# Attention windows fetched in eight-row transfers, and the next batch's transposes and scores placed after the last slot's values

## The chip, the core and the metric

The kernel runs on one core of a Trainium2 chip. Its time is device time in microseconds (us) from the start to the end of the program on that core. The engines are named as the profile names them: PE (TensorE, matrix multiplications; PEld is its weight load), DVE (VectorE), ACT (ScalarE), POOL (GpSimd), SP (SyncE). Every engine works through its own instructions in order. Transfers ("DMAs") are issued by POOL, SP or ACT and carried out by 16 DMA engines that all of them share.

## The reference

Two stages follow each other. First, chunked attention over 4 batches, 8 heads, 768 tokens and a head size of 64. The tokens are cut into chunks of 32; the queries of a chunk see 8 memory keys and values of the batch, plus a window of up to 56 tokens: 16 to the left of the chunk, the chunk, 8 to the right.

```python
scores = scale * np.matmul(q_c, k_full.transpose(0, 1, 3, 2))
a = np.exp(scores - max); a = a / sum(a)
out[:, :, c_start:c_end] = np.matmul(a, v_full)
```

Second, a mixture of 8 experts over the 3072 resulting rows of 512. Two linear maps of a row give noisy logits, the two best experts are chosen, their weights are the softmax of the two logits, and each chosen expert computes `relu(x @ w1) @ w2` with `w1` 512 x 1024 and `w2` 1024 x 512. The result is a 3072 x 512 float32 array.

## The kernel before

Everything is computed in bfloat16 with float32 accumulation; POOL's transfers convert the float32 inputs on the way in.

**Attention** goes through the 4 batches, and through 3 slots for each batch (`i` from 0 to 11, `tp` is the slot within the batch); a slot is 256 tokens, eight chunks. For a batch `b`:

- `load_nat` (L117) loads q, k or v of the batch, one POOL transfer of 768 KB each, into the tiles `nat` (q and k) and `vn` (v). `spread_v` (L368) reorders v into `vp` with two POOL copies. `window_v` then issues from SP a transfer of `vp` to a scratch area `vd` in device memory (L374), and from POOL two transfers of the memory values (L378, 8 partitions each) and four of the windows (L383): for each of two head parities 32 and then 24 window rows. In the resulting tile `vb` the partition is the place in the window (8 memory rows, then 56 window rows; the parities at partitions 0 and 64), so that each of the 24 chunks has its values ready as one operand. A window transfer reads 512-byte pieces of `vd`, since every token occurs in up to two windows.
- `turn` (L393) makes one of eight units of transposed q or k: 12 small PE transposes into a PSUM bank, then a copy to `qT` or `kT` by ACT or DVE. Copies of the four q units are on ACT; the four k units alternate between ACT and DVE (L549).
- `scores` (L408, L415) are 40 matmuls into one PSUM tile `ps_s`, then a row maximum and a subtraction on DVE (L423, L425). `exps` is the exponential on ACT (L430).
- `turn_p` transposes the probabilities on PE and copies them on ACT (L436, L439); `values` computes the row sums (L447) and the weighted values (L453) on PE, and divides on DVE (L457, L460). `turn_x` (L470, L472) and `gate` (L480, L482) are the transposes of the result and the logits; `keep_x` (L485) stores the rows to the area `xd` from ACT.

PE, ACT, DVE and SP follow an order written out by hand, POOL keeps program order. The order in slot `i` is: `scores(i+1)`, `turn_p(i)`, `turn_x(i-1)`, `values(i)`, `exps(i+1)`, `gate(i-1)`, then a part of the routing. A table `PLAN` and the function `fill` put the eight units of the next batch into this: for the first batch all behind the second slot, for the others two q units before that slot's `values` and the rest behind it. Thus the units of the next batch precede the last slot of the current one. At the first slot of a batch POOL issues the window of the next batch, q and k of the one after, the spread of its v, and the load of the v after that.

There is one tile for all experts' weights, `w_all`, 8 places of 16 KB per partition. Attention's buffers (`xrow`, `vn`, both `vb`, four `nat`) lie in the last places, from which an expert is loaded only after attention. The first three experts are loaded by POOL during the last slots (`load_expert`, L78 and L79). Two POOL transfers cannot share one of eight completion counters at the same time, so in the built code each POOL transfer waits for the one issued eight transfers before it, where nothing else already made sure of that.

**Routing and experts.** After the last slot a chain of small DVE, PE and POOL operations sorts the tokens into lists by expert pair. POOL gathers the rows of each list (L671), PE turns the first ones (L691), and then runs all expert matmuls (L714 first layer, L726 second) up to the end, with results scattered to the output by POOL (L677). Other experts' weights are loaded during this stage.

Of the kernel before, what the change touches and what calls it, by code (L numbers as in the profile page):

```python
# [22 lines left out]
def kernel(  # L23
# [40 lines left out]
    w_all = wpool.tile([128, E, WE], BF16, name="w_all")  # L64
    wflat = w_all.rearrange("p e c -> p (e c)")
    w1v = w_all[:, :, 0:KP * F].rearrange("p e (k f) -> p e k f", k=KP)
    w2v = w_all[:, :, KP * F:WE].rearrange("p e (f d) -> p e f d", f=FB)
# [9 lines left out]
    def load_expert(e):  # L77
        pin(nc.gpsimd.dma_start(out=w1v[:, e], in_=moe_w1[e].rearrange("(kp p) f -> p kp f", p=128)))  # L78
        pin(nc.gpsimd.dma_start(out=w2v[:, e], in_=moe_w2[e].rearrange("(fb p) d -> p fb d", p=128)))  # L79


    def load_part(e, i):
        h = slice(i % 2 * KP // 2, (i % 2 + 1) * KP // 2) if i < 2 else slice(i % 2 * FB // 2, (i % 2 + 1) * FB // 2)
        if i < 2:
            pin(nc.gpsimd.dma_start(out=w1v[:, e, h], in_=moe_w1[e].rearrange("(kp p) f -> p kp f", p=128)[:, h]))
        else:
            pin(nc.gpsimd.dma_start(out=w2v[:, e, h], in_=moe_w2[e].rearrange("(fb p) d -> p fb d", p=128)[:, h]))
# [14 lines left out]
    scol = [E * WE]  # L102
# [6 lines left out]
    vb = [scratch(2 * NCH * HP * D).rearrange("p (a c w) -> p a c w", a=2, c=NCH) for _ in range(2)][::-1]  # L109
# [261 lines left out]

    def window_v(b):
        t, o = vb[b % 2], vd[b % 2]
        nc.sync.dma_start(out=o[LC:LC + S, :].rearrange("(p s) c -> p (s c)", s=SO), in_=vp)  # L374
        for par in range(2):
            p0 = par * 64
            cols = slice(par * 256, (par + 1) * 256)
            pin(nc.gpsimd.dma_start(out=t[p0:p0 + NM, par], in_=mvn[b * NM:(b + 1) * NM, cols].unsqueeze(1).to_broadcast([NM, NCH, 256])))  # L378
        for par in range(2):
            p0 = par * 64  # L380
            cols = slice(par * 256, (par + 1) * 256)
            for r0, n in ((0, CH), (CH, WIN - CH)):
                pin(nc.gpsimd.dma_start(out=t[p0 + NM + r0:p0 + NM + r0 + n, par],  # L383
                                        in_=o[r0:r0 + S, cols].rearrange("(c k) w -> k c w", k=CH)[0:n]))
# [131 lines left out]
    with tc.manual_schedule(engines={ET.PE, ET.Activation, ET.DVE, ET.SP}):  # L516
# [10 lines left out]
        spread_v(0)  # L527
        window_v(0)
# [3 lines left out]
        load_v(1)  # L532
        load_kq(1)
        spread_v(1)
# [16 lines left out]
        def fill(i, at):  # L551
            b, tp = divmod(i, TP)
            if b + 1 < B:
                turns(b + 1, PLAN[min(b, 1)].get((tp, at), ()))

# [6 lines left out]
        for i in range(NT):  # L562
# [35 lines left out]
            if last:  # L598
                break
# [386 lines left out]
```

## Time and profile before

| what | us |
|---|---|
| median of 3 runs (lowest, highest) | 363.06 (361.42, 363.59) |
| the profiled execution's own time | 358.42 |
| span of its instructions | 356.7 |
| PE, DVE, ACT, POOL busy | 285.9, 170.3, 136.9, 134.3 |
| start of the last slot's values | 124.51 |
| start of the first expert matmul | 144.14 |

The profiled execution has its own time: it is one run, and the span in its trace leaves out 1.7 us around the instructions. All places in the trace are given in us from the start of the span. A row of a timeline reads: start, duration of the group, engine, line, operation, output <- input, form, how many; in brackets the idle time of that engine just before and what ended it. The table of stretches gives for each stretch of time the busy time of each engine with the number of instructions, the granted PE clock as a share of full speed, the mean share in which the DMA engines had a packet in hand (over 1 where packets overlap) and the GB/s that arrived.

### The profile page before, as it was taken

The page shows a single profiled execution, that of the slowest core. Times are in us where ns is not written, and L with a number is a line of the kernel's source. Part 1 is how long each engine was busy: PE and PEld are TensorE (multiplying, and loading weights), DVE is VectorE, ACT ScalarE, POOL GpSimd, SP SyncE. Part 2 cuts the span into 40 slices and gives each one's busy share as a digit, 9 for nine tenths or more (in the row PEclk, how much of TensorE's full clock was granted, in tenths as well). Part 3 has the DMA queues.
Part 4 walks back from the last instruction along what each step waited for, and adds up shares of the span by engine and source line. Part 5 has one row for each costly group of instructions (what it writes and reads, how often), then busy time and mean ns, then how long its engine had stood idle before and what let it go on. Part 6 is the DMA issues. An engine that isn't in the chain of part 4 may idle for free.

```text
span 356.7 us, 7042 instructions
## 1 busy us (share of the span) xinstructions
PE 285.9 (80%) x2934; PEld 186.3 (52%) x2955; DVE 170.3 (48%) x349; ACT 136.9 (38%) x189; POOL 134.3 (38%) x181
## 2 busy tenths in 40 slices
PE   0356577777847732999999999999999999999991
PEld 0245455666736621865544465664455775565540
DVE  7656456699689885531133302954310334223221
ACT  8813645564645610144322343213243222243310
POOL 6460573354453036706530744332580122201122
PEclk9995655565687865699999999999999999999998
DMA  8999999999999999499999999961289971100012
GB/s 122 235 171 169 245 174 208 251 198 211 247 156 208 253 249 180 106 194 143 178 196 235 209 173 252 159 119 51 87 166 189 208 184 54 53 2 2 25 47 81
DMA packets 49866, 56.97 MB, mean 160 GB/s; under 512 B 16931, under 2 KB 39523, under 8 KB 49828
## 3 DMA queue, kind: packets, MB, share of 16 engines
q0 software_dynamic: 34240, 46.82, 73.2%
q1 hardware_dynamic: 13920, 6.62, 10.9%
q10 hardware_dynamic: 1668, 3.02, 2.4%
q8 instruction: 25, 0.41, 0.5%
q14 instruction: 13, 0.11, 0.1%
HBM read 70.39 MB, written 13.96 MB: 236 GB/s over the span
## 4 chain that ended last, share of the span: by engine, by line
PE 33%; issue 20%; POOL 5%; DVE 4%; DMA 3%; POOLq 1%; ACT 0%; DVEq 0%
PE p_h L714 18%; PE p_y L726 13%; POOL out_dram L677 4%; DMA out_dram<-y,main_dst 1%; DMA xTt<-xt 1%; DMA xt<-xd,main_src 1%; POOL xt L671 1%; DVE w_all L460 1%; PE p_xt L691 0%; POOL w_all L844 0%; POOLq L981 0%; DVE mx L423 0%; DVE sc L425 0%; ACT xT L472 0%; PE ps_o L453 0%
## 5 line engine op out<-in xcount | busy, mean ns | idle before, releaser
L714 PE MATMUL p_h<-xTt,w_all 128*128 128x256 bf16 (+3 forms) x669 | 102.7, 313 | 0.7 <-DVE xTt L692 0.5
L726 PE MATMUL p_y<-w_all,h 128*128 128x512 bf16 x446 | 102.3, 379 | 0.9
L714 PEld LDWEIGHTS <-w_all 128*128 128x128 bf16 x736 | 70.0, 101 | 36.3 <-issue 0.7
L702 ACT ACTIVATE h<-p_h 128x512 bf16<-128x512 f32 (+1 forms) x81 | 44.7, 551 | 95.9 <-PE p_h L714 88.3
L726 PEld LDWEIGHTS <-h 128*128 128x128 bf16 x464 | 45.3, 98 | 51.6
L700 DVE TENSOR_SCALAR h<-p_h 128x512 bf16<-128x512 f32 (+1 forms) x49 | 31.0, 633 | 82.8 <-PE p_h L714 73.7
L677 POOL DMA_INDIRECT out_dram<-y,main_dst x28 | 30.9, 1103 | 87.9 <-DVE y L732 75.4
L732 DVE SCALAR_TENSOR_TENSOR y<-p_y,main_w,y 128x512 f32<-128x512 f32 x28 | 21.0, 750 | 39.2 <-PE p_y L726 32.5
L393 PE MATMUL p_t<-identb,w_all 128*64 128x128 bf16 x384 | 20.6, 288 | 23.0 <-DMA w_all<-in_k_dram 13.4
L671 POOL DMA_INDIRECT xt<-xd,main_src x28 | 27.9, 997 | 24.2 <-DMA xTt<-xt 13.0
L730 ACT ACTIVATE y<-p_y,main_w 128x512 f32<-128x512 f32 x28 | 19.2, 687 | 37.0 <-PE p_y L726 36.0
L393 PEld LDWEIGHTS <-w_all 128*64 128x64 bf16 x384 | 18.1, 155 | 25.2 <-DMA w_all<-in_k_dram 13.9
L439 ACT COPY pT<-p_p 128x1024 bf16<-128x1024 bf16 x12 | 12.1, 1012 | 27.5 <-PE p_p L436 27.5
L383 POOL DMA_DIRECT2D w_all<-vd x16 | 11.8, 747 | 23.8 <-DMA vd<-vp 19.3
L460 DVE TENSOR_TENSOR w_all<-ps_o,rs 128x512 bf16<-128x512 f32 x24 | 15.6, 686 | 8.2 <-PE ps_o L453 7.8
L415 PE MATMUL ps_s<-kT,qT 128*32 128x112 bf16 x384 | 11.6, 276 | 7.2 <-DVE kT L549 5.4
L368 POOL COPY vp<-w_all 128x1536 bf16<-128x1536 bf16 x8 | 11.5, 1469 | 13.2 <-DMA w_all<-in_v_dram 13.2
L430 ACT ACTIVATE pb<-sc 128x1024 bf16<-128x1024 f32 x12 | 12.8, 1063 | 8.9 <-DVE sc L425 8.7
L549 DVE COPY kT<-p_t 64x768 bf16<-64x768 bf16 x12 | 11.5, 955 | 7.9 <-PE p_t L393 7.8
L425 DVE TENSOR_TENSOR sc<-ps_s,mx 128x1024 f32<-128x1024 f32 x12 | 14.7, 1225 | 0.8
L423 DVE TENSOR_REDUCE mx<-ps_s 128x16 f32<-128x1024 f32 x12 | 14.7, 1224 | 0.8 <-PE ps_s L415 0.5
L453 PE MATMUL ps_o<-w_all,pT 128*32 128x128 bf16 x384 | 10.9, 280 | 3.3 <-issue 2.0
(172 smaller groups left out, 284.0 us busy)
## 6 DMA issues: line engine op xcount, KB each, us to landing
w_all<-in_moe_w_dram POOLq DMA_DIRECT2D x16, 1024.0 KB, 20.7
w_all<-in_moe_w_dram POOLq DMA_DIRECT2D x8, 512.0 KB, 13.8
w_all<-in_v_dram POOLq DMA_DIRECT2D x4, 768.0 KB, 12.1
w_all<-in_k_dram POOLq DMA_DIRECT2D x4, 768.0 KB, 20.9
w_all<-in_q_dram POOLq DMA_DIRECT2D x4, 768.0 KB, 18.1
vd<-vp SPq DMA_DIRECT2D x4, 768.0 KB, 9.0
w_all<-vd POOLq DMA_DIRECT2D x8, 384.0 KB, 13.0
w_all<-vd POOLq DMA_DIRECT2D x8, 288.0 KB, 13.3
```

The lines of the kernel that those rows point to most:

```text
L393: nc.tensor.transpose(out=p_t[own(par), s, :], in_=src[:, 2 * pair + par, s * D:(s + 1) * D], identity=identb, tile_position=(0, par * 64))
L423: nc.vector.tensor_reduce(out=mx, in_=s3, axis=AX, op=Alu.max)
L425: nc.vector.tensor_tensor(out=sc, in0=s3, in1=bc(mx, KW), op=Alu.subtract)
L460: nc.vector.tensor_tensor(out=xr[:, j, 0:Dm].rearrange("p (h d) -> p h d", h=H), in0=ps_o[:, j].rearrange("p c a d -> p (c a) d"), in1=bc( ...
L671: i = nc.gpsimd.indirect_dma_start(out=xts[key].bitcast(I32), out_offset=None, in_=xd, in_offset=bass.IndirectOffsetOnAxis(ap=ix, axis=0))
L677: i = nc.gpsimd.indirect_dma_start(out=out, out_offset=bass.IndirectOffsetOnAxis(ap=ix, axis=0), in_=y, in_offset=None, bounds_check=N - 1 ...
L700: nc.vector.tensor_scalar(out=out_, in0=in_, scalar1=0.0, scalar2=None, op0=Alu.max)
L702: nc.scalar.activation(out=out_, in_=in_, func=Act.Relu)
L714: nc.tensor.matmul(out=o, lhsT=w(kp * F + f * 128, 128), rhs=x[:, kp], start=(kp == 0), stop=(kp == KP - 1))
L726: nc.tensor.matmul(out=p, lhsT=h[:, (f * n + j) * 128:(f * n + j + 1) * 128], rhs=w(KP * F + f * Dm, Dm), start=(f == 0), stop=(f == FB - 1))
L730: nc.scalar.activation(out=y, in_=p, func=Act.Copy, scale=weight)
L732: nc.vector.scalar_tensor_tensor(out=y, in0=p, scalar=weight, in1=y, op0=Alu.mult, op1=Alu.add)
```

## The change

Four things change together.

- **Window transfers.** The four window transfers of a batch become 14. Each takes, for one parity, eight rows that lie seven partitions apart (row `x`, `x+7`, ... `x+49` of the window). The transfer of `vp` to `vd` is no longer a part of `window_v`: it follows the spread directly, a batch ahead of its windows.
- **Order on POOL.** The q of the next batch is issued after six of the 14 window transfers, its k after the last. The load of v for the second batch moves ahead of the first window.
- **Places.** Both `vb` tiles become tiles of their own (`w_b`), in which the weights of the last three experts are put later; the remaining attention buffers move to places 2 to 4 of a five-place `w_all`.
- **Order on PE, ACT and DVE.** In the last slot of a batch (`edge`), `scores(i+1)` is no longer at the top. After `values(i)` come `gate(i-1)`, all eight units of the next batch, `scores(i+1)` and `exps(i+1)`. `PLAN` and `fill` are gone. The load of the third expert moves behind the last units.

```diff
-    w_all = wpool.tile([128, E, WE], BF16, name="w_all")
+    EA = E - 3
+    w_all = wpool.tile([128, EA, WE], BF16, name="w_all")
+    w_b = [wpool.tile([128, 3, WP], BF16, name=f"w_b{i}") for i in range(2)]
+    places = [(w_all[:, e, 0:WP], w_all[:, e, WP:WE]) for e in range(EA)]
+    places += [(w_b[2 * x // 3][:, 2 * x % 3], w_b[(2 * x + 1) // 3][:, (2 * x + 1) % 3]) for x in range(3)]
...
-            for r0, n in ((0, CH), (CH, WIN - CH)):
-                pin(nc.gpsimd.dma_start(out=t[p0 + NM + r0:p0 + NM + r0 + n, par],
-                                        in_=o[r0:r0 + S, cols].rearrange("(c k) w -> k c w", k=CH)[0:n]))
+    XW = WIN // 8
+    def spans_v(b, lo, hi):
+        o = vd[b % 2]
+        for x in range(lo, hi):
+            for par in range(2):
+                p0 = par * 64 + NM + x
+                src = bass.AP(tensor=o.tensor, offset=o.offset + x * Dm + par * 256, ap=[[XW * Dm, 8], [CH * Dm, NCH], [1, 256]])
+                pin(nc.gpsimd.dma_start(out=vb[b % 2][p0:p0 + 7 * XW + 1:XW, par], in_=src))
+    def window_v(b):
+        memory_v(b)
+        spans_v(b, 0, 3)
+        if b + 1 < B:
+            load_nat(nat[(b + 1) % 2][1], q, b + 1)
+        spans_v(b, 3, XW)
+        if b + 1 < B:
+            load_nat(nat[(b + 1) % 2][0], k, b + 1)
...
         spread_v(0)
+        copy_v(0)
+        load_v(1)
         window_v(0)
...
-        load_v(1)
-        load_kq(1)
         spread_v(1)
+        copy_v(1)
         load_v(2)
...
             if tp == 0 and more:
                 window_v(b + 1)
                 if b + 2 < B:
-                    load_kq(b + 2)
                     spread_v(b + 2)
+                    copy_v(b + 2)
...
-            if not last:
+            if not (last or edge):
                 sc = scores(i + 1)
...
             xrs[i] = values(i, pTs.pop(i), (lambda: gate(i - 1, xTs_.pop(i - 1))) if last else None)
+            if edge:
+                gate(i - 1, xTs_.pop(i - 1))
+                turns(b + 1, QS + KS)
+                if i == 2 * TP + 2:
+                    load_expert(2)
+                sc = scores(i + 1)
             pbs[i + 1] = exps(sc)
```

54 lines of the change are left out of this document (23 added, 31 removed).

## The prediction

> **What bounds the kernel now.** I read the page's slices first, then the list of waits, then PE's timeline.
>
> ```profile
> span 356.7 us, 7042 instructions
> ...
> DMA  8999999999999999499999999961289971100012
> ```
>
> A slice is 8.9 us. The transfers have work in hand without a break up to slice 16, some 142 us, where attention and routing end. So the span has two parts with different limits, and two stretches show it:
>
> ```profile
> 80.00:100.00 20.00, 15.85 (x356) 13.29 (x355) 16.33 (x35) 12.15 (x16) 9.52 (x17) 0.63 1.19 220
> 144.00:200.00 56.00, 55.60 (x321) 31.94 (x326) 17.78 (x35) 18.31 (x33) 23.14 (x27) 0.95 1.04 182
> ```
>
> From 144 on PE is busy 55.6 of 56 us: the experts' part is PE's own and the change leaves its matmuls alone. Whatever attention gains moves that part earlier by as much, if the first experts' weights are there. In attention no engine is full (DVE 16.3 of 20, PE 15.9), so waits set the pace:
>
> ```profile
> POOL w_all L383 <- DMA vd<-vp: 19.3, 3, 8.9
> PEld L393 <- DMA w_all<-in_k_dram: 13.9, 3, 8.7
> PE p_t L393 <- DMA w_all<-in_k_dram: 13.4, 3, 8.5
> ```
>
> PE waits 13.4 us for k before the transposes of L393 (the same wait again on PEld, its weight load), and POOL 19.3 us for the copy of v to memory before it may issue windows. The timeline places them:
>
> ```profile
> 32.79 1.04 PE L453 MATMUL ps_o<-w_all,pT 128*32 128x128 bf16 x32 [1.30 <-DMA w_all<-vd]
> ...
> 37.36 0.63 PE L453 MATMUL ps_o<-w_all,pT 128*32 128x128 bf16 x32
> ...
> 39.77 2.43 PE L393 MATMUL p_t<-identb,w_all 128*64 128x128 bf16 x48 [1.25 <-DMA w_all<-in_q_dram]
> 45.62 2.13 PE L393 MATMUL p_t<-identb,w_all 128*64 128x128 bf16 x36 [3.43 <-DMA w_all<-in_k_dram]
> 48.16 0.85 PE L393 MATMUL p_t<-identb,w_all 128*64 128x128 bf16 x12 [0.41 <-ACT kT L549]
> ...
> 54.19 1.04 PE L453 MATMUL ps_o<-w_all,pT 128*32 128x128 bf16 x32
> ...
> 80.83 1.04 PE L453 MATMUL ps_o<-w_all,pT 128*32 128x128 bf16 x32
> ...
> 108.72 1.05 PE L453 MATMUL ps_o<-w_all,pT 128*32 128x128 bf16 x32
> ...
> 114.09 0.63 PE L453 MATMUL ps_o<-w_all,pT 128*32 128x128 bf16 x32
> ...
> 120.10 0.63 PE L453 MATMUL ps_o<-w_all,pT 128*32 128x128 bf16 x32
> ...
> 124.51 1.05 PE L453 MATMUL ps_o<-w_all,pT 128*32 128x128 bf16 x32
> ```
>
> I call the start of slot n's values Vn. The rows of L453 are in order V0, V1, V2 (54.19), V5 (80.83), V8 (108.72), V9, V10 and V11 (124.51). Slot 2 has all its own operands at 38, but stands in PE's queue behind the second batch's transposes, which wait for k until 45.62: V1 to V2 takes 16.8 us, against 4.4 us from V10 to V11, where nothing is put between. After that each batch takes 26.6 and 27.9 us.
>
> **The change, part by part.** *Window transfers.* POOL's issues now and the copy's landing:
>
> ```profile
> 13.65 1.36 POOL L378 DMA_DIRECT2D w_all<-mvn  x2 [1.17 <-DVE mvn L526]
> 19.97 2.96 POOL L383 DMA_DIRECT2D w_all<-vd  x4 [4.95 <-DMA vd<-vp]
> ...
> 23.83 0.92 POOL L117 DMA_DIRECT2D w_all<-in_q_dram  x1
> ...
> 51.86 2.88 POOL L368 COPY vp<-w_all 128x1536 bf16<-128x1536 bf16 x2
> vd<-vp SPq DMA_DIRECT2D x1, 768.0 KB, 7.2
> ```
>
> A window transfer of eight rows by 24 pieces isn't in the trace from `vd`, but L378 has the same shape at 0.68 us an issue, and L383 with three to four times the pieces 0.74. 14 of them take 9.5 to 10.4 us where four take 2.96; I use 10.4. That is POOL time, of which there is room: one turn of POOL (windows 10.4, q and k 1.8, spread 2.9, copy 7.2 to land, with the v load and the memory rows inside that wait) is 22.3 us. Windows of batch 0 start at 20 as now, since their copy is as late; with the q load between, their last issue ends at 31.3, and they land near 33 (1.3 us after issue is the least I allow, 3 the most). The first copy lands in 7.2, the median of the four in 9.0. With 7.2 for all, later windows land at 56, 78 and 100, k of the next batches at 37, 59 and 81. With 9.0: 58, 82 and 105.
>
> *Rate of those transfers.* Four stretches of 4 us:
>
> ```profile
> 36.00:40.00 4.00, 2.32 (x64) 1.86 (x64) 3.40 (x6) 2.98 (x3) 3.70 (x3) 0.90 1.31 204
> 48.00:52.00 4.00, 2.66 (x56) 1.97 (x56) 3.13 (x5) 1.70 (x3) 2.68 (x4) 0.50 1.04 145
> 60.00:64.00 4.00, 2.85 (x85) 2.46 (x86) 1.39 (x3) 0.87 (x3) 0.00 (x0) 0.50 1.13 365
> 108.00:112.00 4.00, 3.75 (x99) 3.20 (x97) 3.40 (x8) 2.24 (x3) 2.44 (x1) 0.52 1.15 208
> ```
>
> The last column is GB/s. Plain loads run at 204, windows at 145, the copy of v at 365. A batch's windows (2 x 384 and 2 x 288 KB, 1.38 MB) take 9.5 us at 145 and would take 3.8 at 365: a gain of 0 to 5.7 us of the DMA engines' time a batch. [...] I take a value near the fast end, because issuing (10.4 us) then hides all of it beside the q load; its slow end is a rival below.
>
> *Order on the engines.* With windows landing at 33, V0 is 33.0, V1 37.5 and V2 41.9, from the distances 4.57 (V0 to V1) and 4.41 (V10 to V11) above. Now nothing stands before slot 2. The price is the stretch from V2 to V3, in which nothing else is left to cover the eight units and the softmax that follows them:
>
> ```profile
> 46.52 3.22 ACT L549 COPY kT<-p_t 64x768 bf16<-64x768 bf16 x4 [3.27 <-PE p_t L393]
> 47.16 3.88 DVE L549 COPY kT<-p_t 64x768 bf16<-64x768 bf16 x4 [7.55 <-PE p_t L393]
> L425 DVE TENSOR_TENSOR sc<-ps_s,mx 128x1024 f32<-128x1024 f32 x12 | 14.7, 1225 | 0.8
> L423 DVE TENSOR_REDUCE mx<-ps_s 128x16 f32<-128x1024 f32 x12 | 14.7, 1224 | 0.8 <-PE ps_s L415 0.5
> 55.40 0.36 PE L408 MATMUL ps_s<-mkT,qT 128*128 128x16 bf16 x8
> ...
> 58.75 0.37 PE L447 MATMUL small<-ones,pT 128*128 128x2 bf16 x8 [0.31 <-ACT pT L439]
> ```
>
> Values 1.04 and gate 0.35; six units until DVE has its first k unit, 3.9 (0.61 each in the row at 39.77, 0.85 at 48.16; I take 0.65); DVE's two k units 3.88, beside which ACT's are done; the second half of the scores 0.5; memset, maximum and subtraction 2.65; then, as in the rows from 55.40 to 58.75, the next scores, the transposed probabilities and their copy 3.35, and the sums 0.35. Together 16.0 us. Two further slots take 10.4 (V9 to V11, routing included), so a batch takes 26.4: V3 57.9, V5 68.3, V6 84.3, V8 94.7. These are the times at which windows must be there (56 and 78 land before) and k (59 for the edge at 69).
>
> At the third edge a chain of routing stands in DVE's queue ahead of slot 8's reciprocals, for which `gate(7)` waits, and behind it all units on PE:
>
> ```profile
> 98.10 0.23 DVE L265 TENSOR_TENSOR ns<-ns,nz 128x64 f32<-128x64 f32 x1 [0.61 <-ACT ns L248]
> ...
> 101.46 0.39 DVE L282 TENSOR_TENSOR ohp<-pcode,pc 128x224 bf16<-128x224 f32 x1
> ```
>
> It takes 3.75 us (98.10 to 101.85); slot 8's probabilities and values cover some 1.8 of it, so I add 2.0. V9 is 112.7 (windows at 100), V11 123.1 instead of 124.51: **1.4 us gained** in attention. The change takes away nearly all of the 16.8 and gives most of it back at three uncovered edges.
>
> *First experts.* The gather of the first rows before, and one without a backlog:
>
> ```profile
> 137.47 1.61 POOL L671 DMA_INDIRECT xt<-xd,main_src  x1 [2.24 <-DVE facts L307]
> ...
> xt<-xd,main_src POOLq DMA_INDIRECT x1, 5.5
> ...
> xt<-xd,main_src POOLq DMA_INDIRECT x4, 2.8
> ```
>
> The first gather lands 5.5 us after its issue, with weights still flowing in; the four issued from 142 to 146 need 2.8. Six weight transfers of 1 MB take 30.2 us at the 208 GB/s of the row above. Now they are mixed with windows until 107. Behind the change POOL reaches them at 98, with nothing else to load but two stores of 768 KB (2.2 us each at 365): done by 133, before the gather at 136. **Another 2.7 us**; nothing if POOL is 4 us later.
>
> *Places.* Later experts' loads wait for other buffers than before, but all of attention's readers are done by then; no cost. The third expert's load, behind the edge at 105, is inside the sum just made.
>
> **Sum.** 1.4 + 2.7 = 4.1 us: span 352.6, profiled execution 354.3 instead of 358.42. The median of the runs lies 4.6 us above the profiled execution; I keep that distance: 363.06 - 4.1 = 359.0.
>
> **Rivals.**
>
> *The edges eat the gain.* With PE at half its clock, as in most of attention (0.50 in three of the stretches above), a unit takes the 0.85 of the row at 48.16 instead of 0.65: 1.2 us more at each edge, 3.6 in all, and the later start of everything takes nothing from the gather. That is 359.0 + 3.6 = 362.6, no change. For it: that row. Against it: 48 units' matmuls at 39.77 went at 0.61 a unit.
>
> *Windows no faster.* At 145 GB/s batch 0's windows land near 35.5 instead of 33; all that follows is 2.5 us later, 361.5. Other windows have the slack.
>
> *Slower: eight transfers in flight.* Each POOL transfer waits for the one eight before it. Where a window transfer takes longer to land than eight issues (8 x 0.74 = 5.9 us), POOL goes at the pace of landings and not of issues.
>
> ```profile
> 76.45 0.90 POOL L117 DMA_DIRECT2D w_all<-in_k_dram  x1 [3.42 <-DMA w_all<-in_v_dram]
> w_all<-mvn POOLq DMA_DIRECT2D x8, 96.0 KB, 11.3
> ```
>
> The first row is such a wait today: a k load held 3.42 us by the v load eight transfers earlier. The second is the landing of transfers of the new shape: 11.3 us. At 9 us, 14 windows take 15.8 instead of 10.4, POOL's turn is 27.7, over the 26.4 of a batch, and V3, V6 and V9 slip by 3.4, 1.3 and 1.3; at 11.3 the windows take 19.8, the turn 31.7, and the slips are some 7, 5 and 5. With no gather gain that makes 368 to 379; I write 369. Against it: those landings had two or three loads queued ahead, and the new order leaves one (3.8 us) in front of eight windows. [...]
>
> *More than forecast.* If the two slots behind an edge take 9.0 (4.57 + 4.41) in the first two batches and units 0.61 or less, 3.5 to 5 us more go: 354.5.
>
> **How the numbers follow.** Forecast 0.45 (359.0), edges 0.24 (362.6), windows no faster 0.08 (361.5), slower 0.13 (369), more 0.10 (354.5). The measurement can't tell under 1%, 3.6 us, from no change: limits 359.4 and 366.7. The forecast is just beyond the first, so I count 0.30 of its 0.45 as faster and 0.15 as same; with 0.10 of the last case and 0.03 out of edges and windows, faster is 0.43. Same: 0.15, 0.18 of the edges, 0.07 of the windows, 0.01 of the slow case: 0.41. Slower: 0.12 and 0.04 of the edges: 0.16. The range 354 to 367 leaves out the slow case and half of the fast one; the forecast's own is 356.5 to 361.5.
>
> **What the new profile would show.** V2 near 42, V3 near 58, V5 68, V8 95, V11 123; hardly any wait of PE for k or q; stretches with windows well above 145 GB/s; the first gather landing in about 3 us. Wrong would be: values waiting for windows; POOL's L396 (the new window line) waiting for transfers; V2 to V3 longer than 18 us.

## The result, and the profile after

The change makes the kernel slower: 370.74 us (median of 4 runs, 369.49 to 371.94) against 362.24 us, or 8.5 us more; the ratio is 1.0244, with a 95% interval of 1.0208 to 1.0280. A ratio compares the executions that count as fast alone, so it is not the quotient of the medians. The forecast was 359.0 us, faster. The profiled execution of the changed kernel took 371.94 us, 1.2 above its median, where that of before lay 3.8 below its own; so the two profiles differ by 13.5 us, and some 5 us of that lie in these two executions and not in the medians.

The page of the changed kernel, its span and the busy share of the DMA engines in 40 slices:

```profile
span 370.2 us, 7087 instructions
...
DMA  8999999999959999589999999951289972100012
```

Counted from 0, slice 11 (102 to 111 us), in which POOL issues nothing but window transfers, is at half (5). Before, no slice inside attention is below 8.

PE's timeline of the changed kernel (start, duration, what; in brackets the idle time before and what ended it). L474 is the line of the values, L453 before; the rows are V0, V2, V3, V5, V6, V8, V9, V11, with two waits between them:

```profile
37.94 1.04 PE L474 MATMUL ps_o<-w_b,pT 128*32 128x128 bf16 x32 [6.55 <-DMA w_b<-vd]
...
46.33 0.63 PE L474 MATMUL ps_o<-w_b,pT 128*32 128x128 bf16 x32
...
65.30 1.04 PE L474 MATMUL ps_o<-w_b,pT 128*32 128x128 bf16 x32 [3.43 <-DMA w_b<-vd]
...
76.56 1.04 PE L474 MATMUL ps_o<-w_b,pT 128*32 128x128 bf16 x32
...
93.37 1.04 PE L474 MATMUL ps_o<-w_b,pT 128*32 128x128 bf16 x32 [0.64 <-DMA w_b<-vd]
97.71 1.00 PE L358 MATMUL p_list<-vals,oh_l 128*128 128x168 bf16 x6 [2.98 <-POOL vals L348]
...
106.52 1.05 PE L474 MATMUL ps_o<-w_b,pT 128*32 128x128 bf16 x32
...
124.82 0.63 PE L474 MATMUL ps_o<-w_b,pT 128*32 128x128 bf16 x32
...
134.13 0.77 PE L474 MATMUL ps_o<-w_b,pT 128*32 128x128 bf16 x32
...
151.64 0.58 PE L709 MATMUL p_xt<-identb,xt 128*128 128x128 bf16 x4 [2.79 <-DMA xt<-xd,main_src]
```

| start of | before | forecast | after |
|---|---|---|---|
| V0 | 32.79 | 33.0 | 37.94 |
| V3 | 61.15 | 57.9 | 65.30 |
| V6 | 88.55 | 84.3 | 93.37 |
| V9 | 114.09 | 112.7 | 124.82 |
| V11 | 124.51 | 123.1 | 134.13 |

Behind the start of the program the waits for q and k are gone, as meant; in their place the values wait for windows, 6.55, 3.43 and 0.64 us. V11 is 9.6 us later, and the first rows for the experts are turned 8.6 us later (151.64 against 143.04).

POOL's timeline of the changed kernel says why the windows are late (L396 the window transfers, L123 the loads, L374 the spread, L84 the first experts' weights):

```profile
19.38 3.10 POOL L396 DMA_DIRECT2D w_b<-vd  x5 [4.22 <-DMA vd<-vp]
24.59 0.63 POOL L396 DMA_DIRECT2D w_b<-vd  x1 [2.12 <-DMA w_all<-in_v_dram]
...
33.92 0.63 POOL L396 DMA_DIRECT2D w_b<-vd  x1 [2.63 <-DMA w_all<-in_q_dram]
...
47.52 3.85 POOL L396 DMA_DIRECT2D w_b<-vd  x6 [6.68 <-issue]
51.36 0.93 POOL L123 DMA_DIRECT2D w_all<-in_q_dram  x1
52.28 4.36 POOL L396 DMA_DIRECT2D w_b<-vd  x7
60.37 0.63 POOL L396 DMA_DIRECT2D w_b<-vd  x1 [3.73 <-DMA w_all<-in_q_dram]
60.98 0.93 POOL L123 DMA_DIRECT2D w_all<-in_k_dram  x1
61.91 2.88 POOL L374 COPY vp<-w_all 128x1536 bf16<-128x1536 bf16 x2
...
73.96 3.10 POOL L396 DMA_DIRECT2D w_b<-vd  x5 [6.68 <-DMA vd<-vp]
...
89.75 0.63 POOL L396 DMA_DIRECT2D w_b<-vd  x1 [5.09 <-DMA w_all<-in_q_dram]
...
103.17 8.68 POOL L396 DMA_DIRECT2D w_b<-vd  x14 [4.27 <-DMA vd<-vp]
111.85 0.81 POOL L84 DMA_DIRECT2D w_all<-in_moe_w_dram  x1
```

The last window transfer of each of the first three windows waits for the q load that stands eight POOL transfers before it: 2.63, 3.73 and 5.09 us. A turn of POOL, from one window's first issue to the next one's, takes 28.1, 26.4 and 29.2 us instead of 22.3. The first window is also held for v, 2.12 us. The last 14 transfers, which have no load among them, take 8.68 us, 0.62 each.

### The profile page after: what moved, and what is told of

It reads as the page before. It is cut to its first block, busy times and chain, and to the rows that moved or that the text cites. A ratio compares the mean times of both kernels' runs of the same rounds, so it can differ in the third digit from the quotient of the medians.

```text
span 370.2 us, 7087 instructions
## 1 busy us (share of the span) xinstructions
PE 284.9 (77%) x2934; PEld 183.8 (50%) x2955; DVE 167.4 (45%) x349; ACT 136.8 (37%) x189; POOL 157.4 (42%) x221
## 4 chain that ended last, share of the span: by engine, by line
issue 26%; PE 22%; POOL 8%; DVE 5%; DMA 2%; POOLq 1%; ACT 1%; ACTq 0%; DVEq 0%
PE p_h L732 11%; PE p_y L744 9%; POOL out_dram L695 6%; POOL xt L689 2%; DMA out_dram<-y,main_dst 1%; DVE w_all L481 1%; DMA xt<-xd,main_src 1%; PE p_xt L709 0%; DVE y L750 0%; DVE h L718 0%; DVE mx L444 0%; DVE sc L446 0%; POOLq L999 0%; ACT xT L493 0%; POOL w_all L862 0%
## 5 line engine op out<-in xcount | busy, mean ns | idle before, releaser
L732 PE MATMUL p_h<-xTt,w_all 128*128 128x384 bf16 (+3 forms) x381 | 65.1, 331 | 2.8 <-issue 2.1
L744 PE MATMUL p_y<-w_all,h 128*128 128x512 bf16 x285 | 65.6, 379 | 2.2 <-ACT y L748 1.6
L732 PEld LDWEIGHTS <-w_all 128*128 128x128 bf16 x448 | 41.6, 101 | 29.3 <-issue 2.9
L396 POOL DMA_DIRECT2D w_b<-vd x56 | 34.8, 629 | 36.2 <-DMA vd<-vp 15.2
L732 PE MATMUL p_h<-xTt,w_b 128*128 128x256 bf16 (+1 forms) x288 | 38.0, 290 | 0.0
L744 PE MATMUL p_y<-w_b,h 128*128 128x512 bf16 x161 | 36.9, 379 | 0.4
L689 POOL DMA_INDIRECT xt<-xd,main_src x28 | 27.9, 998 | 21.7 <-DMA xTt<-xt 8.2
L732 PEld LDWEIGHTS <-w_b 128*128 128x128 bf16 x288 | 28.1, 98 | 9.9
L414 PE MATMUL p_t<-identb,w_all 128*64 128x128 bf16 x384 | 19.3, 272 | 15.2 <-DMA w_all<-in_k_dram 8.7
L414 PEld LDWEIGHTS <-w_all 128*64 128x64 bf16 x384 | 16.8, 146 | 17.2 <-DMA w_all<-in_k_dram 8.8
L481 DVE TENSOR_TENSOR w_all<-ps_o,rs 128x512 bf16<-128x512 f32 x24 | 15.5, 686 | 14.7 <-PE ps_o L474 14.0
L474 PE MATMUL ps_o<-w_b,pT 128*32 128x128 bf16 x384 | 10.4, 267 | 11.9 <-DMA w_b<-vd 10.6
```

The lines of the kernel that those rows point to most:

```text
L396: pin(nc.gpsimd.dma_start(out=vb[b % 2][p0:p0 + 7 * XW + 1:XW, par], in_=src))
L414: nc.tensor.transpose(out=p_t[own(par), s, :], in_=src[:, 2 * pair + par, s * D:(s + 1) * D], identity=identb, tile_position=(0, par * 64))
L481: nc.vector.tensor_tensor(out=xr[:, j, 0:Dm].rearrange("p (h d) -> p h d", h=H), in0=ps_o[:, j].rearrange("p c a d -> p (c a) d"), in1=bc( ...
L689: i = nc.gpsimd.indirect_dma_start(out=xts[key].bitcast(I32), out_offset=None, in_=xd, in_offset=bass.IndirectOffsetOnAxis(ap=ix, axis=0))
L732: nc.tensor.matmul(out=o, lhsT=w(kp * F + f * 128, 128), rhs=x[:, kp], start=(kp == 0), stop=(kp == KP - 1))
L744: nc.tensor.matmul(out=p, lhsT=h[:, (f * n + j) * 128:(f * n + j + 1) * 128], rhs=w(KP * F + f * Dm, Dm), start=(f == 0), stop=(f == FB - 1))
```

## The experiments

Four theories stood against each other at different times: *transfers* (14 issues hold POOL up), *load order* (the loads that were moved), *edges* (the uncovered stretch behind each last slot) and *places in the tile* (how far apart the rows of a transfer are). "Four" stands for the four old window transfers. Every ratio is to runs of the kernel before beside it on the same chip.

| run | places | windows | loads | order | ratio (95% interval) |
|---|---|---|---|---|---|
| own_tiles | new | four | old | old | 0.999 (0.996, 1.002) |
| order_only | old | four | old | new | 1.0003 (0.9947, 1.0059) |
| loads_only | new | four | moved | old | 1.0032 (0.9983, 1.0081) |
| four_again | new | four | moved | new | 1.0261 (1.0174, 1.0349) |
| own_seven_apart | new | 14 | old | old | 1.0212 (1.0159, 1.0264) |
| own_seven_alternate | new | 14 | old | old | 1.0196 (1.0108, 1.0284) |
| own_seven_new_order | new | 14 | old | new | 1.0179 (1.0108, 1.0249) |
| transfers_only | new | 14 | moved | old | 1.0151 (1.0104, 1.0199) |
| changed kernel | new | 14 | moved | new | 1.0244 (1.0208, 1.0280) |
| loads_behind | new | 14 | v ahead, q and k behind | new | 1.0114 (1.0021, 1.0207) |
| v_back | new | 14 | v behind window 0 | new | 1.0418 (1.0230, 1.0606) |
| near_rows | new | 14, neighbours | moved | new | 1.0495 (1.0373, 1.0617) |
| own_two_apart | new | 4, two apart | old | old | 0.9963 (0.9937, 0.9990) |
| own_two_apart_new_order | new | 4, two apart | old | new | 0.9950 (0.9917, 0.9983) |
| own_four_apart | new | 8, four apart | old | old | 0.9855 (0.9796, 0.9914) |
| two_apart | old | 4, two apart | old | old | 1.0788 (1.0653, 1.0923) |
| two_apart_new_order | old | 4, two apart | old | new | 1.0750 (1.0623, 1.0876) |
| sync_seven | new | 14 from SP | old | old | 1.1739 (1.1665, 1.1812) |
| sync_seven_new_order | new | 14 from SP | old | new | 1.1547 (1.1476, 1.1617) |

**The order, with and without the transfers and loads.** `order_only` is before with this edit:

```diff
-            if not last:
+            if not (last or edge):
                 sc = scores(i + 1)
...
+            if edge:
+                gate(i - 1, xTs_.pop(i - 1))
+                turns(b + 1, QS + KS)
...
+                sc = scores(i + 1)
             pbs[i + 1] = exps(sc)
```

> The kernel before with only the new order on PE, ACT and DVE: units, scores and softmax of the next batch behind the last slot's values, the third expert's load behind them. Transfers, loads and places stay as they were. Theory 'transfers' (the changed kernel is slow because its windows land late, most of its 8.5 us): within 2 us of before, ratio 0.995 to 1.006, V11 (start of the last slot's values) 122 to 127. Theory 'edges' (the three uncovered edges are what costs): 6 to 9 us slower, ratio 1.016 to 1.025, V11 131 to 134 with no wait of values for a window.

`transfers_only` is the changed kernel with that edit taken back.

> The changed kernel with the old order on PE, ACT and DVE put back: 14 window transfers, loads between them, tiles of their own stay. Theory 'transfers': still 4 to 8 us slower than before, ratio 1.011 to 1.022, and V0 and V3 wait for windows by 3 to 7 us. Theory 'edges': within 2 us of before, ratio 0.995 to 1.006.

The order alone is level, and without it most of the loss stays. PE's timeline of `order_only` (L453 the values; the rows are V2, V3, V6 and V11):

```profile
41.08 0.63 PE L453 MATMUL ps_o<-w_all,pT 128*32 128x128 bf16 x32
...
62.12 1.04 PE L453 MATMUL ps_o<-w_all,pT 128*32 128x128 bf16 x32 [4.70 <-issue]
...
89.85 0.63 PE L453 MATMUL ps_o<-w_all,pT 128*32 128x128 bf16 x32
...
126.41 0.73 PE L453 MATMUL ps_o<-w_all,pT 128*32 128x128 bf16 x32
```

The rows of V3 and V6 in the timeline of before:

```profile
61.15 1.04 PE L453 MATMUL ps_o<-w_all,pT 128*32 128x128 bf16 x32 [2.03 <-issue]
...
88.55 1.04 PE L453 MATMUL ps_o<-w_all,pT 128*32 128x128 bf16 x32
```

V2 comes 13 us earlier than before (54.19), and V3 not at all: PE stands 4.70 us ahead of it, where it stood 2.03 before. These two rows don't name what ended the wait; slot 3 is the first that needs the second window, and where the profile of a later run names it, it is the window. So the k wait in slot 2, which looked like the bound, lay beside another one.

**The places alone**, `own_tiles`:

```diff
-    w_all = wpool.tile([128, E, WE], BF16, name="w_all")
...
+    w_all = wpool.tile([128, EA, WE], BF16, name="w_all")
+    w_b = [wpool.tile([128, 3, WP], BF16, name=f"w_b{i}") for i in range(2)]
```

> The kernel before with only the places changed: both window tiles are tiles of their own, with the last three experts' weights in them later. Transfers, loads and the order of the engines are those of before. Every theory: no difference, ratio 0.994 to 1.006, V0 32.8, V11 124 to 126. If the places cost something by themselves (a later expert's load that waits for another buffer), it shows as more than 2 us behind 145.

As expected, nothing in the time. In its profile V3 is at 63.69 and V11 at 126.04, though, 2.5 and 1.5 us later than in that of before: places in two profiles can differ by this much without a cause in the edit, and the ratios decide.

**The transfers alone.** `own_seven_apart`, seven of one parity and then seven of the other, and `own_seven_alternate`, alternating as in the changed kernel; `window_v` itself and the loads stay where they were:

```diff
-            for r0, n in ((0, CH), (CH, WIN - CH)):
-                pin(nc.gpsimd.dma_start(out=t[p0 + NM + r0:p0 + NM + r0 + n, par], ...))
+            for x in range(7):
...
+                pin(nc.gpsimd.dma_start(out=t[p0 + NM + x:p0 + NM + x + WIN - 7 + 1:7, par], in_=src))
```

> Places and transfers alone: tiles of their own and the 14 window transfers of eight rows seven apart, but v, q and k issued behind the whole window as before, and the old order of the engines. Theory 'load order' (the moved loads are what makes the changed kernel slow): V0 31 to 33.5, no wait of a window transfer for a q load, ratio 0.985 to 1.005. Theory 'number' (14 small transfers, each waiting for the one eight before, hold POOL up wherever the loads are): ratio 1.008 to 1.020, like the 1.015 of the changed transfers and loads with the old order.

> As own_seven_apart (places and 14 transfers, loads behind them, old order), but the two parities alternate as in the changed kernel. If seven transfers of one parity in a row were what made that run 1.021: ratio 0.995 to 1.008 and no waits of a window transfer for an earlier one. If the number and the wait for the transfer eight before are the cause: 1.015 to 1.027 again.

The number costs 2% with no load moved, and the order of parities isn't the reason. A stretch of before in which the first window passes, with the first of the loads behind it (a ninth of the bytes, by the packets in the trace; the last three numbers are PE's clock, the DMA engines' share and GB/s; the fifth pair is POOL's busy time):

```profile
24.00:30.00 6.00, 3.98 (x93) 3.31 (x93) 4.48 (x10) 1.06 (x1) 1.62 (x2) 0.71 1.12 156
```

The same stretch of `own_seven_alternate`:

```profile
24.00:30.00 6.00, 3.99 (x93) 3.31 (x93) 4.49 (x10) 1.09 (x2) 6.00 (x11) 0.72 0.57 160
```

POOL's timeline of `own_seven_alternate`, the first window:

```profile
21.73 8.72 POOL L389 DMA_DIRECT2D w_b<-vd  x14 [6.49 <-DMA vd<-vp]
```

And PE's timeline of it, the transposes of the next q:

```profile
43.88 2.77 PE L398 MATMUL p_t<-identb,w_all 128*64 128x128 bf16 x48 [5.36 <-DMA w_all<-in_q_dram]
```

This pair of stretches is the core of the case. 156 GB/s pass before and 160 now, but the DMA engines have a packet in hand for a share of 1.12 there and of 0.57 here, and POOL is busy for all 6.00 us. Rows apart halve the engines' work (a 4 KB packet of a window takes 0.40 us on average there and 0.22 here), and the engines idle for the other half, because 96 KB per issue of 0.623 us is 158 GB/s.

A rival is that a transfer of eight rows can use only some of the engines, and that these are full. The packets of the trace speak against it: taken in order, the bytes of each of the 14 transfers are in 1.5 to 1.8 us after its issue, 1.6 for the first and 1.8 for the last, so next to nothing piles up behind the issues. In the last window of `near_rows` below, where the engines are full, the same lag grows from 1.5 to 6.5 us.

The loads that before were already queued behind the window are issued 5.8 us later (the 8.72 against 2.96 us of issues), and PE waits 5.36 us for q, where it waited 1.25 before.

**The loads.** `loads_only` and `four_again` have the old four transfers among the moved loads, in the old and in the new order:

```diff
         memory_v(b)
-        spans_v(b, 0, 3)
+        rows_v(b, 0, CH)
         load_nat(nat[(b + 1) % 2][1], q, b + 1)
-        spans_v(b, 3, XW)
+        rows_v(b, CH, WIN - CH)
         load_nat(nat[(b + 1) % 2][0], k, b + 1)
```

> The changed kernel with the four window transfers of 32 and 24 rows again, the q load between the two pairs and k behind them, all else as changed. If 14 transfers instead of four are what makes the windows late, V0 falls from 37.9 to 33 to 35, POOL reaches the next spread 6 us earlier in each batch, and the ratio to before is 0.995 to 1.010. If the load order (v of the second batch ahead of the first window, q in the middle) is the cause whatever the transfers' size, V0 stays at 36 to 38 and the ratio at 1.015 to 1.025.

> Places and the moved loads alone: four window transfers of 32 and 24 neighbouring rows, v of the second batch ahead of window 0, q between the two pairs of window transfers, k behind them, copy of v behind the spread; old order of the engines. With the new order these gave 1.026. Theory 'load order': V0 40 to 42 again, ratio 1.015 to 1.027. If only the new order made them dear (it waits for windows where the old one waits for k): 1.000 to 1.010.

V0 is 3.4 to 4.0 us later in both than in the changed kernel: the v load and q stand ahead of the last two long transfers. So with these loads four long transfers bring the first window no earlier than 14 small ones, and V0 of `four_again` is beyond the 36 to 38 expected of the load order. In the old order the time is level with before all the same (though V11 is at 131.19 in the one execution profiled), and in the new one it isn't. PE's timeline of `loads_only`, rows V0, V3, V6 and V11:

```profile
41.94 1.04 PE L471 MATMUL ps_o<-w_b,pT 128*32 128x128 bf16 x32 [10.87 <-DMA w_b<-vd]
...
67.13 0.63 PE L471 MATMUL ps_o<-w_b,pT 128*32 128x128 bf16 x32 [1.10 <-issue]
...
92.16 0.63 PE L471 MATMUL ps_o<-w_b,pT 128*32 128x128 bf16 x32
...
131.19 1.05 PE L471 MATMUL ps_o<-w_b,pT 128*32 128x128 bf16 x32
```

The same rows of `four_again`:

```profile
41.31 1.05 PE L471 MATMUL ps_o<-w_b,pT 128*32 128x128 bf16 x32 [10.42 <-DMA w_b<-vd]
...
69.12 1.05 PE L471 MATMUL ps_o<-w_b,pT 128*32 128x128 bf16 x32
...
99.06 1.04 PE L471 MATMUL ps_o<-w_b,pT 128*32 128x128 bf16 x32
...
136.66 1.05 PE L471 MATMUL ps_o<-w_b,pT 128*32 128x128 bf16 x32
```

From V3 to V6 the old order takes 25.0 us and the new one 29.9. With 14 transfers and the old loads the new order is level with the old one (1.0179 and 1.0196):

> Places, 14 transfers with alternating parities, loads behind them as before, new order of PE, ACT and DVE; the changed kernel without its moved loads. If the new order is dear only where windows are late for slot 0 and 3 (moved loads): V0 32.8, V3 62 to 64, ratio 1.010 to 1.020, level with or below the 1.0196 of the old order. If the order itself costs with 14 transfers, because POOL's late loads and routing operations then meet an edge that covers nothing: 1.022 to 1.035.

**The wait for the transfer eight before.** `loads_behind`:

```diff
-        spans_v(b, 0, 3)
+        spans_v(b, 0, XW)
         load_nat(nat[(b + 1) % 2][1], q, b + 1)
-        spans_v(b, 3, XW)
         load_nat(nat[(b + 1) % 2][0], k, b + 1)
```

> The changed kernel with one edit: q and k of the next batch are both issued behind all 14 window transfers. If the last of 14 waits for the q load eight transfers earlier (2.6 to 5.1 us each time in the changed kernel), that wait goes, the last window of each batch is issued 3 to 6 us earlier and lands 4 to 7 us earlier; V0 32.5 to 35 instead of 37.9, V3's wait of 3.4 us is gone, and the time falls by 4 to 8 us against the changed kernel: ratio to before 1.000 to 1.013. If the transfers are slow in themselves and not by the load among them, V0 stays at 37 or later and the ratio at 1.018 or more.

V0 falls by 4.1 us to 33.80 and V11 to 129.88, as the theory said. The ratio goes from 1.0244 to 1.0114, about half of the loss, though the interval reaches from nearly all of it to a sixth. The edit takes away the wait and also the load's own bytes ahead of the last transfers; no run separates the two. The second window is still waited for, in PE's timeline of `loads_behind`:

```profile
61.14 1.04 PE L473 MATMUL ps_o<-w_b,pT 128*32 128x128 bf16 x32 [1.15 <-DMA w_b<-vd]
```

In POOL's timeline of it, the sixth transfer of that window now waits for v instead:

```profile
52.73 5.64 POOL L396 DMA_DIRECT2D w_b<-vd  x9 [3.63 <-DMA w_all<-in_v_dram]
```

`v_back` puts the v load of the second batch behind window 0 again:

```diff
         copy_v(0)
-        load_v(1)
         window_v(0)
...
+        load_v(1)
         spread_v(1)
```

> The changed kernel with one edit: the load of v for the second batch goes back behind window 0 (behind its q and k too). The wait of 2.1 us of the sixth window transfer goes, and V0 falls from 37.9 to 34 to 36. If only window 0 counts, the time falls by 2 to 4 us (ratio to before 1.013 to 1.019). If the chain v load, spread, copy, window 1 counts as much, the second spread waits for v until some 42, window 1 is issued 3 to 6 us later than at 47.5, V3 is 66 to 71 instead of 65.3, and the ratio is 1.024 to 1.035.

The second outcome, and more than it said: V0 only falls to 37.41, and V3 is at 74.67 in PE's timeline of `v_back`:

```profile
74.67 1.04 PE L474 MATMUL ps_o<-w_b,pT 128*32 128x128 bf16 x32 [13.33 <-DMA w_b<-vd]
```

So with q and k among the windows, v can't be issued behind them: the turn of v load, spread, copy and window then sets V3. It doesn't follow that v had to go ahead of the window: in `own_seven_alternate` v stands behind the 14 transfers but ahead of q and k, and V3 is at 63.41.

**How far apart the rows are.** `near_rows` keeps all of the change but takes eight neighbouring rows:

```diff
-                p0 = par * 64 + NM + x
+                p0 = par * 64 + NM + 8 * x
...
-                pin(nc.gpsimd.dma_start(out=vb[b % 2][p0:p0 + 7 * XW + 1:XW, par], in_=src))
+                pin(nc.gpsimd.dma_start(out=vb[b % 2][p0:p0 + 8, par], in_=src))
```

> The changed kernel with eight neighbouring rows in each of the 14 window transfers instead of eight rows seven apart; number, size and place of the transfers stay. Theory 'places in the tile' (rows seven apart are written faster): window packets take longer (0.4 us and more instead of 0.22 to 0.33), the windows land 1 to 4 us later each time, the kernel is 2 to 6 us slower than the changed one (ratio to before 1.030 to 1.040). Theory 'issue' (POOL issues 96 KB per 0.627 us, 157 GB/s, and that is the limit whatever the rows): within 2 us of the changed kernel, ratio 1.019 to 1.030.

A stretch of `near_rows` in which only windows pass:

```profile
36.00:40.00 4.00, 0.00 (x0) 0.00 (x0) 0.00 (x0) 0.00 (x0) 1.87 (x3) 1.00 1.09 99
```

And one of the changed kernel:

```profile
106.00:110.00 4.00, 2.01 (x56) 1.81 (x58) 3.52 (x16) 1.07 (x2) 4.00 (x8) 0.50 0.56 156
```

99 GB/s with the engines' share at 1.09 against 156 at 0.56: eight neighbours cost the engines three times as much per byte. The ratio, 1.0495, is above what the theory of the places expected (1.030 to 1.040), with an interval that reaches into it.

Why rows apart take less of the engines' time stays open: no run shows it.

`two_apart` takes four transfers of 28 rows two apart in the tile of before; `own_two_apart` does so in tiles of its own; both also with the new order:

```diff
+            for x in range(2):
...
+                pin(nc.gpsimd.dma_start(out=t[p0 + NM + x:p0 + NM + x + WIN - 1:2, par], in_=src))
```

> The kernel before with one edit: the four window transfers of a batch take 28 rows two apart each, instead of 32 and 24 neighbouring ones; four issues, the old loads, the old order of the engines. Theory 'places in the tile': window packets take about 0.25 us instead of 0.40 to 0.46, a batch's windows pass 3 to 4 us faster, V0 is 30 to 31.5 instead of 32.8, V3 57 to 60 instead of 61.2, and the kernel is 2 to 6 us faster than before (ratio 0.983 to 0.995). If the rows' distance does nothing: ratio 0.996 to 1.004 and V0 at 32.8.

> The same four transfers of rows two apart, with the new order of PE, ACT and DVE (units, scores and softmax behind the last slot's values) and the old loads. The new order alone left the time as it was, with slot 3 waiting 4.7 us for its window (V3 62.1). If the transfers are what held it, V3 comes to 57 to 59, V11 to 117 to 122 instead of 126.4, and the ratio to before is 0.970 to 0.990, below that of the same transfers in the old order. If the uncovered edges hold it, V11 stays above 123 and the ratio is 0.995 to 1.005, above that of the old order.

> Places, and four window transfers of 28 rows two apart in the old load order and the old order of the engines. In the shared tile these transfers made a row store of ACT wait 28 us for windows; in tiles of their own that wait should be gone (it was an order kept between parts of one tile). Then, if rows two apart pass as little faster as the window 0 of that run (V0 32.0 instead of 32.8): ratio 0.990 to 1.002. If the 28 us wait comes back, the ratio is above 1.05 and the tile was not its cause.

> The same with the new order of PE, ACT and DVE. With the old windows the new order was level (1.000), slot 3 waiting for its window until 62.1. Theory 'transfers hold slot 3': V3 58 to 61, V11 121 to 125, ratio 0.985 to 0.998. Theory 'edges eat it': V11 126 or later, ratio 0.998 to 1.006.

In the shared tile both were some 8% slower, for a reason that the first two expectations did not have. ACT's timeline of `two_apart`:

```profile
85.56 0.37 ACTq L485 DMA_DIRECT2D xd<-w_all  x1
86.02 1.01 ACT L472 COPY xT<-p_x 128x1024 bf16<-128x1024 bf16 x1 [28.07 <-DMA w_all<-vd]
```

The store of finished rows out of `w_all` waits for windows written into other columns of `w_all`, and with it ACT stands for 28.07 us. In tiles of their own the same transfers are 0.4% faster than before; the wait is gone. That is what the places are for: without them rows two apart cost 8%. Rows seven or four apart were not run in the shared tile. Also, the new order adds nothing that the intervals don't cover (0.9950 and 0.9963).

**Four apart.** Eight transfers of 14 rows, everything else old but the places:

```diff
+            for x in range(4):
...
+                pin(nc.gpsimd.dma_start(out=t[p0 + NM + x:p0 + NM + x + WIN - 4 + 1:4, par], in_=src))
```

> Places and eight window transfers of 14 rows four apart, old loads, old order. Four transfers of rows two apart gave 0.996, 14 of rows seven apart 1.020 (own_seven_alternate). Theory 'number on POOL's queue': eight issues of about 0.65 us take 5.2 us instead of 3.0 and 8.7, the loads behind them are 2.2 us later than with four; ratio 1.000 to 1.011, V0 31.5 to 33. Theory 'small or scattered pieces pass slowly': V0 33 or later and 1.012 or more. If rows further apart pass faster and the number costs nothing up to eight: 0.985 to 0.996.

355.08 us against 359.27 (medians), ratio 0.9855 (0.9796 to 0.9914): faster than both kernels. POOL's timeline of it, the first window, 168 KB an issue:

```profile
20.59 5.00 POOL L390 DMA_DIRECT2D w_b<-vd  x8 [5.39 <-DMA vd<-vp]
```

A stretch in which its second window passes:

```profile
50.00:56.00 6.00, 5.01 (x124) 4.31 (x123) 4.53 (x7) 2.88 (x3) 4.37 (x6) 0.50 1.04 172
```

PE's timeline of it, rows V3, V6 and V11:

```profile
59.27 0.63 PE L459 MATMUL ps_o<-w_b,pT 128*32 128x128 bf16 x32 [0.58 <-DMA w_b<-vd]
...
84.31 1.04 PE L459 MATMUL ps_o<-w_b,pT 128*32 128x128 bf16 x32
...
122.69 0.63 PE L459 MATMUL ps_o<-w_b,pT 128*32 128x128 bf16 x32
```

Eight issues in 5.00 us let 275 GB/s through (8 x 168 KB), the engines are full (1.04) and move 172 GB/s: here the issue isn't the limit. V3 is 1.9 us earlier than before and V11 1.8 (4.4 and 3.4 earlier than in `own_tiles`). Why eight beat four by 1% isn't settled: no run separates the distance of the rows from the size of the transfers there.

**Issued by SP.** `sync_seven` and `sync_seven_new_order` are `own_seven_alternate` with SP as issuer:

```diff
-                pin(nc.gpsimd.dma_start(out=t[p0:p0 + WIN - 6:7, par], in_=src))
+                nc.sync.dma_start(out=t[p0:p0 + WIN - 6:7, par], in_=src)
```

> As own_seven_alternate, but the 14 window transfers are issued by SP, behind the copy of v that SP issues anyway; POOL issues only memory rows, loads and weights. Theory 'POOL's queue' (0.627 us an issue and eight in flight hold the windows up): windows land 2 to 6 us earlier, V0 30 to 32, V3 55 to 60, ratio 0.970 to 0.998, below own_seven_alternate by 1 to 3%. Theory 'slow in themselves': no better than own_seven_alternate, 1.010 or more. SP's own time for an issue is not known from the runs; if it is over 0.7 us, the first theory loses its gain.

> The same with the new order of PE, ACT and DVE. If windows are in time (before 57 for V3), the price of the edge (15.5 us from V2 to the sums of slot 3 in the changed kernel) sets V3: 56 to 58, V11 117 to 123, and the ratio is 0.965 to 0.990, below sync_seven by 0.5 to 1.5%. If the edges give back all that the order gains: equal to sync_seven within 0.5%.

The first 14 issues take SP 25.55 us (SP's timeline of `sync_seven`), 1.82 us on average, and V0 is at 58.84:

```profile
19.72 25.55 SPq L389 DMA_DIRECT2D w_b<-vd  x14
```

This is not SP's own time for an issue. The single ones take from 0.65 to 4.97 us there, while POOL's next loads of v, q and k fill the engines (a share of 1.26 from 20 to 45 us); in the third window all 14 take 0.65 to 0.68 us, about as long as on POOL. In each of the later windows SP stands still among the 14 until a store of finished rows that ACT issued has landed, says its list of waits (total, times, longest):

```profile
SPq L389 <- DMA xd<-w_all: 52.9, 3, 25.8
```

So these runs are slow by what the transfers meet on the way, and an issue of over 0.7 us of SP's own, the condition named in the expectation, isn't shown. They say nothing of what the transfers cost on a queue that issues them undisturbed.

## Why the prediction was wrong

**What bounds the kernel.** The forecast read attention as set by waits, and took k before slot 2 as the one to remove. `order_only` removes it and gains nothing, since slot 3 is held until 62.12 all the same. The row of V3 in before, shown above, has such a wait too (2.03 us); the prediction did not use it. It also read more into the list of waits than was there: of the 13.4 us of PE for k, 8.54 lie at the start, where the first batch comes in, and stay. This is PE's timeline of before and then of the changed kernel:

```profile
13.89 2.13 PE L393 MATMUL p_t<-identb,w_all 128*64 128x128 bf16 x36 [8.54 <-DMA w_all<-in_k_dram]
...
14.04 2.13 PE L414 MATMUL p_t<-identb,w_all 128*64 128x128 bf16 x36 [8.71 <-DMA w_all<-in_k_dram]
```

**Window transfers: the step that failed.** The term "one turn of POOL ... is 22.3 us" came out as 26.4 in the turn from 47.52 to 73.96. By its parts: issues 8.84 (forecast 10.4), q and k 1.86 (1.8), spread 2.88 (2.9), the wait for q 3.73 (0), and from the spread's end to the copy's landing 9.17 (7.2). An issue was cheaper than its bounds of 0.68 and 0.74 us. What was missing is the wait, which I had only as a rival, and the copy's landing was taken at its best. The first window is late before any such turn: its issues were to end at 31.3 and end at 34.55, because POOL waits 2.12 us for v, 0.79 for memory values and 2.63 for q among them. The 1.3 to 3 us that I allowed from there to the landing were my own bounds; V0 starts 3.39 us behind it, at 37.94. So windows were there at 37.9, 65.3 and 93.4, where 33, 56 and 78 stood, and the weights were reached at 111.85, where 98 stood. All three signs that the prediction named for being wrong are there: values wait for windows, L396 waits for transfers, and V2 to V3 takes 19.0 us.

The same part put the longer issuing at nothing, as "POOL time, of which there is room". `own_seven_alternate` shows that it costs even with the loads behind it: while POOL issues small transfers, nothing else is queued and the engines are at 0.57.

**Rate.** That rows seven apart would pass near the fast end of 145 to 365 GB/s was my estimate, and no run shows it: 160 GB/s pass in `own_seven_alternate`. Right in kind is that they need half of the engines' time (a share of 0.57 against 1.12). But I had written the gain into the time without asking what 14 issues let through: 14 x 96 KB in 8.7 us is 158 GB/s, no more than the 156 of before. The 365 GB/s taken for the fast end was also misread as the copy of v: 4 us at that rate are 1.46 MB, and the copy has 0.79; a store of rows and loads pass in the same stretch.

**Order on the engines.** Its sizes held: from V2 to V3 without the wait for the window 15.5 us (65.30 - 3.43 - 46.33) against 16.0; from V8 to V9 18.3 against 18.0. But a batch was put at 26.4 against 26.6 to 27.9 before, and those hold transfer waits. From V3 to V6 the new order takes longer than the old one in each of five pairs of runs: 27.7 against 27.4 (`order_only`, before), 27.6 against 26.6 (`own_two_apart_new_order`, `own_two_apart`), 32.8 against 28.1 (`own_seven_new_order`, `own_seven_alternate`), 29.9 against 25.0 (`four_again`, `loads_only`) and 28.1 against 25.0 (changed kernel, `transfers_only`). Waits for transfers are in all of these, so what the edge costs alone isn't separated. With windows from POOL the order gains in no pair of runs more than the intervals cover, and with moved loads it loses (1.0032 to 1.0261, 1.0151 to 1.0244).

**The 11.0 us by which V11 missed its forecast** are, along the rows above: V0 +4.9, its window's wait at V3 +3.4 and at V6 +0.6, and 3.0 at 97.71, where the routing's lists wait for POOL's `vals`, queued behind the late loads: a late queue of POOL reaching PE in a way I had not named. The rest are differences of under 1.2 us each that come to about -1.

**First experts.** Of the 2.7 us 1.0 came: from V11 to the first turned rows 17.5 us instead of 18.5.

**Places.** No cost: right.

**The rivals.** *Eight transfers in flight* had 0.13, and its 369 is near the 370.7 measured, but by another price: not windows that take 9 to 11 us to land, but a load among them that holds the transfer eight places behind it. That the number came out near is luck. The load among the windows is about half of the loss, within a wide interval (`loads_behind`). 14 issues cost the 2% of `own_seven_alternate` where no load stands among them, though some there still wait for a load issued ahead of them (1.63 us for v in the second window), and the two aren't additive. What counts for these transfers of 96 KB is the issuer's 0.62 us: from the first issue at 21.73 to V0 at 32.78, `own_seven_alternate` took 11.1 us for 14 of them, several in flight at a time (an issue every 0.62 us, and 3.6 us from issue to landing in the median of all 56). *The edges eat the gain* has the time of `order_only`, no change, but its price didn't show: at the first edge of the changed kernel three units take 1.20 us, 0.40 each, and at the third edge seven take 4.61, 0.66 each, not 0.85. *Windows no faster* is what the rate of 160 against 156 amounts to, but the delay of 2.5 us that it counted is smaller than the 4.9 of V0.

## What to carry to other kernels

A faster transfer is only worth its bytes per issue: divide the size by the issuer's time for one issue and compare with what passes now, before counting a gain (here 96 KB in 0.62 us, 158 GB/s, against 156). When many small transfers replace a few large ones, whatever was queued behind them starts later by the added issuing time (5.8 us in `own_seven_alternate`), and where each transfer waits for the one eight before it, a large load holds a small one behind it (by 2.63 to 5.09 us in the changed kernel). Removing the longest wait of one engine gains nothing while another chain ends at the same place (`order_only`, 1.0003); find the second wait at the next point where the two meet.

## What the runs showed of the hardware that I had not expected

- Rows seven partitions apart use 0.57 of the DMA engines for 160 GB/s, 32 and 24 neighbours 1.12 for 156 (a ninth of it loads), eight neighbours 1.09 for 99. Between these the choice of rows is worth a factor of two to three in engine time per byte.
- POOL takes 0.62 us to issue a transfer of eight rows by 24 pieces (96 KB) and 0.63 for one of 14 rows (168 KB); SP takes 0.65 for the first kind where nothing holds it (third window of `sync_seven`).
- The order of the loads alone moves V0 from 32.41 (`own_tiles`) to 41.94 (`loads_only`), with the same transfers.
- The first experts' stage differs by run: from the first expert matmul to the end of the span the changed kernel's profile has 217.5 us, before 212.6 and `order_only` 210.6. Over the profiles of all runs with the new places it is 211.2 to 217.5, and 210.6 to 212.6 with the old ones; since `own_tiles` is level with before over ten executions, I count this to the single executions, which no run proves.
